# First batch's softmax sums moved from TensorE to GpSimd and VectorE, and the weight rounding spread over more slots, in a one-core attention and Fourier kernel

## The chip, the core and the metric

The kernel runs on one core of one Trainium2 chip. The core has five engines that work side by side, each through its own list of instructions in order: TensorE (PE: matrix products, results in PSUM), VectorE (DVE), ScalarE (ACT), GpSimd (POOL) and SyncE (SP, which here only issues transfers). An instruction that must wait for another engine holds up all behind it on its own engine. The metric is device time in microseconds; the kernel before takes 1061.83 us, the median of three runs (1060.62 to 1062.22).

## The reference

Inputs are q, k and v of 4 batches, 8 heads, 768 positions and 64 features, a table of sampled blocks, and two weight matrices of 512 x 2048 and 2048 x 512. For each batch and head:

```python
scores = scale * q @ k.T                     # 768 x 768
scores = where(mask, scores, -1e9)           # window, first and last block, 3 sampled blocks
attn = exp(scores - max) ; attn = attn / sum(attn)
x = attn @ v                                 # heads side by side: 768 x 512
mixed = real(fft over positions and features of x)
u = x + mixed ; un = normalised rows of u
out = u + maximum(un @ w_ch1, 0) @ w_ch2
```

## The kernel before, in words

Two heads make a pair; there are 16 pairs, four a batch. A pair is worked on in 12 units: two halves of 384 query positions, each with six chunks `c` of 128 key positions. For a unit TensorE makes the scores of both heads (`scores`, L573, 128 keys x 384 queries each), ScalarE takes their exponentials into a tile `e` (`weigh`, L593; four such tiles, 128 x 768), and TensorE multiplies `e` with v (`values`, L647). Two units are a slot, three slots a half pair, six a pair, 24 a batch (`SB`). `slot(sl)` writes the instructions of one slot: scores of this slot, values of the slot before, and what else fits. In the early slots the mask is added by four small TensorE products (L583); later VectorE multiplies with a mask tile instead (L603). The switch comes when the first batch's mixing has been written out.

The softmax sums. For the second batch and later, `gather` adds up the `e` tiles of a half pair into a tile `acc`: five additions, either one VectorE instruction (L628) or two GpSimd instructions, one per head (L633), whichever a small clock in the planner says is ready sooner. Per pair, `total` (L720 to L731) then lets TensorE sum `acc` over its partitions into a PSUM tile `sp`, and VectorE adds that to `sums` (`into_sums`, L696 and L698). For the first batch, `add_up` (L700 to L718) lets TensorE sum the `e` tiles themselves, in every slot, with eight-record products of 32 rows (L714), kept in PSUM over a half pair. `norm_steps` turns the sums over and inverts them.

The weights arrive as 64-bit floats in 32 chunks of 512 KB (`w_load`, L451, on SyncE's queue) into raw tiles and are rounded to 32 bits by `w_round`: two ScalarE instructions (L460, L463) and five VectorE instructions (L464, L466, L469, L471, L472). Five raw tiles ("rooms" 0, 1, 3, 4, 5 of a shared buffer) go around. `w_steps` writes `W_PACE * sl` roundings by slot `sl`. The same rooms later hold what the mixing needs: rooms 0 and 1 the folded x, rooms 2 and 3 the hidden activations, rooms 4 and 5 differences for a product scheme with seven multiplications instead of eight. SyncE's queue also carries q, k, v and the tables of cosines and sines, whose landing tiles VectorE frees by copying them out (L389, L414).

When a batch's attention is done, its mixing is written into the next batch's slots by `begin`: VectorE scales x (L756) and folds it (L779 to L807), TensorE transforms it (`along`, L827 to L855, writes `zp`; `across` writes `pq`), VectorE and GpSimd normalise, TensorE transposes (L970) and VectorE makes differences (L1007). Then the channel products (`quad`, L1045, and `channels`, L1101) are placed between attention slots. The planner keeps estimates of each engine's time in `when` and writes a step when it expects its inputs; nothing is reordered on the chip. PSUM tiles have tags: `s` (2, scores), `o` (1, values), `m` (2) and `t` (1). `add_up` uses `m`, `total` and the transposes `xt` (L670) and `tp` (L506) use `t`.

Of the kernel before, what the change touches and what calls it, by code (L numbers as in the profile page):

```python
# [11 lines left out]
FP32 = mybir.dt.float32  # L12
# [3 lines left out]
U32 = mybir.dt.uint32  # L16
AX = mybir.AxisListType
ALU = mybir.AluOpType
# [84 lines left out]
def kernel(  # L103
# [14 lines left out]
    nc = tc.nc  # L118

    B, H, S, D = q.shape  # L120
    DM = H * D
    FF = w_ch1.shape[1]
    P = 128
    C = S // P
    BLK = 32
    NB = S // BLK
    NR = sampled_blocks.shape[1]
    HS = S // 2
# [9 lines left out]
    NP = H // 2  # L138
# [20 lines left out]
    pick = const.tile([P, 2 * BLK], FP32, name="pick")  # L159
# [16 lines left out]
    sum_p = ctx.enter_context(tc.tile_pool(name="sum_p", bufs=1))  # L176
# [3 lines left out]
    un_p = ctx.enter_context(tc.tile_pool(name="un_p", bufs=3))  # L180
# [4 lines left out]
    ps_m = ctx.enter_context(tc.tile_pool(name="ps_m", bufs=2, space=PSUM))  # L185
# [3 lines left out]
    when = {"PE": 0.0, "ACT": 0.0, "DVE": 0.0, "POOL": 0.0}  # L189
    free = {"m": [0.0, 0.0], "t": [0.0]}  # L190

    def busy(engine, us, after=0.0):
        when[engine] = max(when[engine], after) + us
        return when[engine]

    def bank(tag):

        at = free[tag].index(min(free[tag]))
        when["PE"] = max(when["PE"], free[tag][at])
        free[tag][at] = float("inf")  # L200
        return tag, at

    def give(which, at):
        free[which[0]][which[1]] = at + HOP

    HOP = 0.1

    def room(i, shape, name, dtype=FP32):
        return big.tile(shape, dtype, tag=f"big{i}", name=name)

    pairs = [(b, j) for b in range(B) for j in range(NP)]
# [84 lines left out]
    def bit(n):  # L296
# [5 lines left out]
                      in_=bass.AP(tensor=_words(sampled_blocks, NB * NR), offset=0,  # L302
                                  ap=[[0, NB], [1, 2 * NB * NR]]))
# [132 lines left out]
    WN = 512  # L436
    wchunks = []
# [6 lines left out]
                              ap=[[2 * cols, P], [1, 2 * WN]])  # L444
                wchunks.append((src, w_sb[:, row, col:col + WN]))
    wraw = {}
    W_ROOMS = (0, 1, 3, 4, 5)

    def w_load(i):
        t = room(W_ROOMS[i % len(W_ROOMS)], [P, 3 * WN], "wraw", U32)  # L450
        nc.sync.dma_start(out=t[:, 0:2 * WN].bitcast(I32), in_=wchunks[i][0])  # L451
        wraw[i] = t

# [28 lines left out]
    by_pe, to_gather = set(), deque()  # L482
    masks = {"by_pe": True}

    turned, e_of, acc_of, o_of, sums_of, x_of, sp_of = {}, {}, {}, {}, {}, {}, {}
    s_at, e_at, e_free, oT_at, acc_at = {}, {}, {}, {}, {}

    def turn_on(n, a, half):
# [63 lines left out]
    UP = 2 * C  # L552
    UNITS = len(pairs) * UP
    SLOT = 2
# [32 lines left out]
    def weigh(u, s):  # L587
        n, w = divmod(u, UP)
        half, c = divmod(w, C)
        e = ep.tile([P, 2, HS], FP32, tag="e", name="e")  # L590
        e_of[u] = e
        if u in by_pe:
            nc.scalar.activation(out=e, in_=s[:, :, 0:HS], func=ACT.Exp, scale=scale)  # L593
            e_at[u] = busy("ACT", 0.8, max(s_at[u], e_free.pop(u - 2 * SLOT, 0.0))) + HOP
            if n >= NP:
                to_gather.append(u)

            if w >= UP - SLOT:
                gather_to(u)
        else:  # L600
            nc.scalar.activation(out=s[:, :, 0:HS], in_=s[:, :, 0:HS], func=ACT.Exp, scale=scale)  # L601
            m = mask[:, c, half * HS:(half + 1) * HS].rearrange("p (o s) -> p o s", o=1)
            nc.vector.tensor_tensor(out=e, in0=s[:, :, 0:HS], in1=m.broadcast_to([P, 2, HS]),  # L603
                                    op=ALU.mult)
            e_at[u] = busy("DVE", 0.97, busy("ACT", 0.8, s_at[u]) + HOP) + HOP
            gather_to(u)
            if n >= NP:
                gather(u)
# [5 lines left out]
    def gather(u):  # L614


        n, w = divmod(u, UP)
        half, c = divmod(w, C)
        if c == 0:
            return  # L620
        if c == 1:
            acc_of[n, half] = acc_p.tile([P, 2, HS], FP32, tag="acc", name="acc")
        acc, e = acc_of[n, half], e_of[u]
        start = e_of[u - 1] if c == 1 else acc
        at = max(e_at[u], acc_at.get((n, half), 0.0))
        sooner = max(when["DVE"], at) + 1.0 < max(when["POOL"], at) + 2.9
        if u in by_pe and masks["by_pe"] and w < UP - SLOT and sooner:
            nc.vector.tensor_tensor(out=acc, in0=start, in1=e, op=ALU.add)  # L628
            acc_at[n, half] = busy("DVE", 1.0, at) + HOP
        else:  # L630

            for i in range(2):
                nc.gpsimd.tensor_add(out=acc[:, i, :], in0=start[:, i, :], in1=e[:, i, :])  # L633
            acc_at[n, half] = busy("POOL", 2.9, at) + HOP
        e_free[u] = acc_at[n, half]

    def values(u):
# [51 lines left out]

    def into_sums(key, j, sp):  # L690
        if j == 0:
            if key == (0, 1):
                sums_of[key] = un_p.tile([P, DM], FP32, tag="un", name="sums")[:, 0:HS]
            else:
                sums_of[key] = sum_p.tile([P, HS], FP32, tag="sums", name="sums")
            nc.vector.tensor_copy(out=sums_of[key], in_=sp)  # L696
        else:
            nc.vector.tensor_tensor(out=sums_of[key], in0=sp, in1=sums_of[key], op=ALU.add)  # L698

    def add_up(us):  # L700


        n, w = divmod(us[0], UP)
        half, c = divmod(w, C)
        j = pairs[n][1]
        if c == 0:
            sp_of[n, half] = ps_m.tile([P, 512], FP32, tag="m", name="sp"), bank("m")
        sp, at = sp_of[n, half]
        sp = sp[:, 0:HS]
        busy("PE", 0.85)  # L710
        for r, u in enumerate(us):
            for i in range(2):
                g = BLK * (2 * i + r)
                nc.tensor.matmul(sp[g:g + BLK, :], pick[:, BLK - j:2 * BLK - j], e_of[u][:, i, :],  # L714
                                 start=(c == 0), stop=(c == C - SLOT), tile_position=(0, g))
        if c == C - SLOT:
            into_sums((0, half), j, sp)
            give(at, busy("DVE", 0.6, when["PE"] + HOP))  # L718

    def total(n):  # L720

# [11 lines left out]
    def norm_steps(b):  # L733

        r = sm.tile([P, T, 4, NP], FP32, tag="r", name="r", bufs=2)

        def invert(half):
            sums = sums_of.pop((0, half) if b == 0 else b)
            st = ps_t.tile([P, T, 4, BLK], FP32, tag="t", name="st")
            for c in range(T):  # L740
                nc.tensor.transpose(st[:, c, :, :].rearrange("p g r -> p (g r)"),
                                    sums[:, c * P:(c + 1) * P], ident)
            if b > 0:
                nc.vector.reciprocal(out=r, in_=st[:, :, :, 0:NP])
                return
            for i in range(2):
                to = r[:, :, 2 * half + i, :]
                nc.vector.tensor_copy(out=to, in_=st[:, :, 2 * i, 0:NP])
                nc.vector.tensor_tensor(out=to, in0=st[:, :, 2 * i + 1, 0:NP], in1=to, op=ALU.add)
            if half == 1:  # L750
                nc.vector.reciprocal(out=r, in_=r)

        def scale_x(half, c):
            xc = x_of[b, half][:, c, :].rearrange("p (j i d) -> p j i d", i=2, d=D)
            rc = r[:, c, 2 * half:2 * half + 2, :].rearrange("p i (j o) -> p j i o", o=1)
            nc.vector.tensor_tensor(out=xc, in0=xc, in1=rc.broadcast_to([P, NP, 2, D]),  # L756
                                    op=ALU.mult)

        return ([("t", lambda h=h: invert(h), 0.45, 0.0, 0.9) for h in range(2 if b == 0 else 1)] +
                [("d", lambda h=h, c=c: scale_x(h, c), 0.0, 0.0, 0.9)  # L760
                 for h in range(2) for c in range(T)])

# [484 lines left out]
    LEAVES = 9.0  # L1247
    SP = UP // SLOT
    SB = SP * NP
    W_PACE = 1.42  # L1250
    short, apart, late, due = deque(), deque(), deque(), deque()
    asked = set()
    needed = set()
    state = {"paired": False, "total": None, "w": 0, "got": 0, "owed": 0.0, "ready": 0.0}
# [89 lines left out]
        return True  # L1344

    def w_loads():
        while state["got"] < min(len(wchunks), state["w"] + len(W_ROOMS)):
            w_load(state["got"])
            state["got"] += 1

# [5 lines left out]
    def slot(sl):  # L1356
        phase, r = divmod(sl, SB)
# [6 lines left out]
        def sum_up():  # L1364

            at = due.popleft()
            done = range(SLOT * at, SLOT * at + SLOT)
            for u in done:
                values(u)
            if at < SB:  # L1370
                add_up(done)
            for u in done:
                e_of.pop(u)

# [47 lines left out]
        if sl < B * SB and n % NP == 1 and s == 1:  # L1422
# [3 lines left out]
                until(lambda: (b - 2, 1) in finished)  # L1426
                at = when["PE"] + LEAVES
            short.append(("t", at, lambda: place(n - 1, 1)))
        if sl > SB and s == 0 and sl <= B * SB:
            short.append(("t", acc_at[n - 1, 1], lambda: total(n - 1)))  # L1430
            state["total"] = short[-1]
        if r == 0:
# [186 lines left out]
```

## Time and profile before

| what | value |
|---|---|
| median of three runs | 1061.83 us (1060.62 to 1062.22) |
| profiled execution: span, first to last instruction | 1059.7 us |
| profiled execution: its own device time | not given beside the span |
| TensorE busy | 1036.7 us, mean granted clock 0.995 |
| VectorE, ScalarE, GpSimd busy | 654.7, 374.3, 235.6 us |
| slots 3 to 24 (20.63 to 123.33 us) | 102.70 us: TensorE busy 99.25, VectorE 92.87, ScalarE 88.36, GpSimd 0.00 |
| slots 24 to 33 (123.33 to 158.00 us) | 34.67 us: TensorE 34.18, VectorE 31.81, ScalarE 20.79, GpSimd 24.18 |

A line of the timeline gives the start in us from the span's start, the duration, the engine, the line of the kernel, the operation, the tiles (written, then read), the shape, how many instructions were merged, and in brackets the idle time before it with what ended it. TensorE's float products are recorded twice each, so eight records stand for four products. A line of a table by stretches gives the stretch, its length, busy time and instructions of TensorE, TensorE's weight loads, VectorE, ScalarE and GpSimd, then the granted TensorE clock, the transfers' share and GB/s.

### The profile page before, as it was taken

The page shows a single profiled execution, that of the slowest core. Times are in us where ns is not written, and L with a number is a line of the kernel's source. Part 1 is how long each engine was busy: PE and PEld are TensorE (multiplying, and loading weights), DVE is VectorE, ACT ScalarE, POOL GpSimd, SP SyncE. Part 2 cuts the span into 40 slices and gives each one's busy share as a digit, 9 for nine tenths or more (in the row PEclk, how much of TensorE's full clock was granted, in tenths as well). Part 3 has the DMA queues.
Part 4 walks back from the last instruction along what each step waited for, and adds up shares of the span by engine and source line. Part 5 has one row for each costly group of instructions (what it writes and reads, how often), then busy time and mean ns, then how long its engine had stood idle before and what let it go on. Part 6 is the DMA issues. An engine that isn't in the chain of part 4 may idle for free.

```text
span 1059.7 us, 12422 instructions
## 1 busy us (share of the span) xinstructions
PE 1036.7 (98%) x4390; PEld 535.8 (51%) x4390; DVE 654.7 (62%) x1218; ACT 374.3 (35%) x742; POOL 235.6 (22%) x262
## 2 busy tenths in 40 slices
PE   8999999999999999999999999999999999999996
PEld 4333345444455554444444555444445554578575
DVE  6898894667645445664668364765457455575663
ACT  6978855664030112342441302253220211210210
POOL 1000183537000002454553001256520001000000
PEclk9999999999999999999999999999999999999998
DMA  7757422220000002212220001221000001000001
GB/s 214 231 168 232 117 46 45 45 47 15 1 0 1 1 0 48 59 29 54 42 54 2 1 0 30 60 38 28 11 11 6 1 0 32 29 0 1 1 20 43
DMA packets 120803, 46.65 MB, mean 44 GB/s; under 512 B 108176, under 2 KB 113822, under 8 KB 120734
## 3 DMA queue, kind: packets, MB, share of 16 engines
q1 hardware_dynamic: 119484, 45.06, 17.3%
q10 hardware_dynamic: 1218, 0.72, 0.3%
q8 instruction: 36, 0.59, 0.2%
q14 instruction: 33, 0.27, 0.1%
q0 software_dynamic: 32, 0.01, 0.0%
HBM read 37.11 MB, written 6.29 MB: 41 GB/s over the span
## 4 chain that ended last, share of the span: by engine, by line
PE 89%; DVE 4%; DMA 3%; ACT 2%; issue 1%; SPq 0%; POOL 0%; ACTq 0%; DVEq 0%
PE y L1101 23%; PE z L1045 15%; PE s L573 12%; PE o L647 10%; PE yp L1045 7%; PE yy L1164 7%; PE xp L1045 4%; PE zp L855 2%; DMA out_dram<-x 1%; PE s L583 1%; PE zp L827 1%; PE sp L714 1%; PE sp L728 1%; PE utp L970 1%; PE xt L670 1%
## 5 line engine op out<-in xcount | busy, mean ns | idle before, releaser
L633 POOL TENSOR_TENSOR acc<-acc,e 128x384 f32<-128x384 f32 x158 | 159.3, 1042 | 94.1 <-DVE e L603 75.1
L573 PE MATMUL s<-qT,kT 64*128 64x384 f32 x768 | 154.0, 516 | 7.7 <-ACT e L593 4.3
L647 PE MATMUL o<-e,vr 128*64 128x384 f32 x768 | 141.8, 497 | 0.0
L1101 PE MATMUL y<-w_sb,hB 128*128 128x512 f32 x288 | 128.2, 596 | 1.0 <-DVE x L1104 1.0
L1101 PE MATMUL y<-w_sb,hA 128*128 128x512 f32 x288 | 128.4, 595 | 0.0
L603 DVE TENSOR_TENSOR e<-s,mask 128x768 f32<-128x768 f32 x92 | 83.8, 951 | 57.6 <-ACT s L601 47.8
L1104 DVE TENSOR_TENSOR x<-y,x 128x512 f32<-128x512 f32 x72 | 49.7, 690 | 110.9 <-PE y L1101 110.8
L573 PEld LDWEIGHTS s<-qT,kT 64*128 64x128 f32 x768 | 64.2, 186 | 85.8 <-issue 22.1
L601 ACT ACTIVATE s<-s 128x768 f32<-128x768 f32 x92 | 69.9, 792 | 87.5 <-PE s L573 87.0
L1045 PE MATMUL z<-unT,t 128*128 128x384 f32 x256 | 93.1, 486 | 1.2 <-DVE hA L1050 1.2
L633 POOL TENSOR_TENSOR acc<-e 128x384 f32<-128x384 f32 x42 | 47.1, 1142 | 211.6 <-ACT e L593 126.7
L1050 DVE TENSOR_TENSOR hA<-z,hA 128x384 f32<-128x384 f32 x64 | 35.7, 557 | 87.5 <-PE z L1045 87.5
L593 ACT ACTIVATE e<-s 128x768 f32<-128x768 f32 x100 | 76.1, 815 | 36.2 <-PE s L583 31.2
L1101 PEld LDWEIGHTS y<-w_sb,hB 128*128 128x128 f32 x288 | 53.4, 190 | 67.7 <-issue 65.0
L918 POOL TENSOR_SCALAR st<-st 128x1 f32<-128x1 f32 x24 | 8.6, 358 | 346.9 <-DVE st L917 346.8
L1101 PEld LDWEIGHTS y<-w_sb,hA 128*128 128x128 f32 x288 | 53.3, 190 | 62.8 <-issue 59.7
L647 PEld LDWEIGHTS o<-e,vr 128*64 128x64 f32 x768 | 47.9, 136 | 70.3 <-issue 67.9
L1054 ACT ACTIVATE hA<-hA 128x384 f32<-128x384 f32 x64 | 33.5, 523 | 120.3 <-DVE hA L1050 119.9
L1045 PEld LDWEIGHTS z<-unT,t 128*128 128x128 f32 x256 | 48.5, 190 | 35.5 <-DVE hA L1050 2.1
L1054 ACT ACTIVATE hB<-hB 128x384 f32<-128x384 f32 x64 | 33.5, 523 | 86.5 <-DVE hB L1050 84.2
L1065 ACT COPY hA<-xp 128x384 f32<-128x384 f32 x32 | 15.3, 478 | 97.9 <-PE xp L1045 97.9
L1045 PE MATMUL xp<-unT,w_sb 128*128 128x384 f32 x128 | 47.2, 492 | 0.0
(202 smaller groups left out, 1428.7 us busy)
## 6 DMA issues: line engine op xcount, KB each, us to landing
wraw<-in_moe_w_ch_dram SPq DMA_DIRECT2D x32, 512.0 KB
vr<-in_v_dram SPq DMA_DIRECT2D x30, 192.0 KB
qb<-in_q_dram SPq DMA_DIRECT2D x44, 96.0 KB
kb<-in_k_dram SPq DMA_DIRECT2D x44, 96.0 KB
x<-oT SPq DMA_DIRECT2D x192, 12.0 KB
out_dram<-x SPq DMA_DIRECT2D x15, 128.0 KB
out_dram<-x SPq DMA_DIRECT2D x7, 256.0 KB
qr<-in_q_dram SPq DMA_DIRECT2D x24, 64.0 KB
```

The lines of the kernel that those rows point to most:

```text
L573: nc.tensor.matmul(s[:, i, 0:HS], kT[rows, c * P:(c + 1) * P], qT[rows, queries], start=True, stop=u not in by_pe)
L593: nc.scalar.activation(out=e, in_=s[:, :, 0:HS], func=ACT.Exp, scale=scale)
L601: nc.scalar.activation(out=s[:, :, 0:HS], in_=s[:, :, 0:HS], func=ACT.Exp, scale=scale)
L603: nc.vector.tensor_tensor(out=e, in0=s[:, :, 0:HS], in1=m.broadcast_to([P, 2, HS]), op=ALU.mult)
L633: nc.gpsimd.tensor_add(out=acc[:, i, :], in0=start[:, i, :], in1=e[:, i, :])
L647: nc.tensor.matmul(o[D * i:D * i + D, :], vt[:, i, c, :], e[:, i, :], start=(c == 0), stop=(c == C - 1))
L1045: nc.tensor.matmul(to, a[:, k, :], c[:, k, :], start=(k == 0), stop=(k == ND // 2 - 1))
L1050: tt(out=to, in0=ps, in1=a, op=ALU.add)
L1054: nc.scalar.activation(out=h, in_=h, func=ACT.Relu)
L1101: nc.tensor.matmul(y, hs[0, half][:, l, m * P:(m + 1) * P], w2_sb[:, 4 * r + l, :], start=(l == 0), stop=(l == 3))
L1104: nc.vector.tensor_tensor(out=x[:, m, :], in0=y, in1=x[:, m, :], op=ALU.add)
L1164: nc.tensor.matmul(ps, a[:, k, :], c[k // 2][:, k % 2, :] if isinstance(c, list) else c[:, k, :], start=(k == 0), stop=(k == 3))
```

## The change

The first batch's sums are made like the others': `add_up` and its special cases go, every unit's `e` goes through `gather`, and `total` runs for every pair. The planner's price for a GpSimd addition goes from 2.9 to 2.2. The weight rounding goes from 1.42 chunks a slot to one, so it ends some eight slots into the second batch, and chunks from the twentieth on use only rooms 3, 4 and 5, since the mixing wants rooms 0 and 1 then.

```diff
     wraw = {}
-    W_ROOMS = (0, 1, 3, 4, 5)
+    W_FREE = 20
+    W_ROOMS = [(0, 1, 3, 4, 5)[i % 5] if i < W_FREE else (3, 4, 5)[(i - W_FREE) % 3]
+               for i in range(len(wchunks))]
...
             e_at[u] = busy("ACT", 0.8, max(s_at[u], e_free.pop(u - 2 * SLOT, 0.0))) + HOP
-            if n >= NP:
-                to_gather.append(u)
+            to_gather.append(u)
...
-        sooner = max(when["DVE"], at) + 1.0 < max(when["POOL"], at) + 2.9
+        sooner = max(when["DVE"], at) + 1.0 < max(when["POOL"], at) + 2.2
...
-            acc_at[n, half] = busy("POOL", 2.9, at) + HOP
+            acc_at[n, half] = busy("POOL", 2.2, at) + HOP
...
-    def add_up(us):
-        n, w = divmod(us[0], UP)
-        half, c = divmod(w, C)
-        j = pairs[n][1]
-        if c == 0:
-            sp_of[n, half] = ps_m.tile([P, 512], FP32, tag="m", name="sp"), bank("m")
-        sp, at = sp_of[n, half]
-        sp = sp[:, 0:HS]
-        busy("PE", 0.85)
-        for r, u in enumerate(us):
-            for i in range(2):
-                g = BLK * (2 * i + r)
-                nc.tensor.matmul(sp[g:g + BLK, :], pick[:, BLK - j:2 * BLK - j], e_of[u][:, i, :],
-                                 start=(c == 0), stop=(c == C - SLOT), tile_position=(0, g))
-        if c == C - SLOT:
-            into_sums((0, half), j, sp)
-            give(at, busy("DVE", 0.6, when["PE"] + HOP))
...
-            sums = sums_of.pop((0, half) if b == 0 else b)
+            sums = sums_of.pop(b)
...
-    W_PACE = 1.42
+    W_PACE = 1.0
...
     def w_loads():
-        while state["got"] < min(len(wchunks), state["w"] + len(W_ROOMS)):
+        while (state["got"] < len(wchunks) and
+               W_ROOMS[state["got"]] not in W_ROOMS[state["w"]:state["got"]]):
             w_load(state["got"])
...
-            if at < SB:
-                add_up(done)
...
-        if sl > SB and s == 0 and sl <= B * SB:
+        if 0 < sl <= B * SB and s == 0:
             short.append(("t", acc_at[n - 1, 1], lambda: total(n - 1)))
```

More of the change, by code (lines that the diff above doesn't have):

```diff
@@ L446 @@
     wraw = {}
-    W_ROOMS = (0, 1, 3, 4, 5)
+    W_FREE = 20
+    W_ROOMS = [(0, 1, 3, 4, 5)[i % 5] if i < W_FREE else (3, 4, 5)[(i - W_FREE) % 3]
+               for i in range(len(wchunks))]
     def w_load(i):
-        t = room(W_ROOMS[i % len(W_ROOMS)], [P, 3 * WN], "wraw", U32)
+        t = room(W_ROOMS[i], [P, 3 * WN], "wraw", U32)
         nc.sync.dma_start(out=t[:, 0:2 * WN].bitcast(I32), in_=wchunks[i][0])
@@ L483 @@
     masks = {"by_pe": True}
-    turned, e_of, acc_of, o_of, sums_of, x_of, sp_of = {}, {}, {}, {}, {}, {}, {}
+    turned, e_of, acc_of, o_of, sums_of, x_of = {}, {}, {}, {}, {}, {}
     s_at, e_at, e_free, oT_at, acc_at = {}, {}, {}, {}, {}
@@ L691, in into_sums @@
         if j == 0:
[L692 to L695, printed above, removed]
+            sums_of[key] = sum_p.tile([P, HS], FP32, tag="sums", name="sums")
             nc.vector.tensor_copy(out=sums_of[key], in_=sp)
@@ L735, in norm_steps, with invert @@
         r = sm.tile([P, T, 4, NP], FP32, tag="r", name="r", bufs=2)
-        def invert(half):
-            sums = sums_of.pop((0, half) if b == 0 else b)
+        def invert():
+            sums = sums_of.pop(b)
             st = ps_t.tile([P, T, 4, BLK], FP32, tag="t", name="st")
@@ L742, in invert @@
                                     sums[:, c * P:(c + 1) * P], ident)
[L743 to L751, printed above, removed]
+            nc.vector.reciprocal(out=r, in_=st[:, :, :, 0:NP])
         def scale_x(half, c):
@@ L757, in scale_x @@
                                     op=ALU.mult)
-        return ([("t", lambda h=h: invert(h), 0.45, 0.0, 0.9) for h in range(2 if b == 0 else 1)] +
+        return ([("t", invert, 0.45, 0.0, 0.9)] +
                 [("d", lambda h=h, c=c: scale_x(h, c), 0.0, 0.0, 0.9)
```

## The prediction

> **What bounds the kernel now.** I read the page's busy shares, then the timelines of TensorE, VectorE and GpSimd in the first batch, then the longest stall there.
>
> ```profile
> PE 1036.7 (98%) x4390; PEld 535.8 (51%) x4390; DVE 654.7 (62%) x1218; ACT 374.3 (35%) x742; POOL 235.6 (22%) x262
> 85.46 1.56 PE L573 MATMUL s<-qT,kT 64*128 64x384 f32 x8
> ...
> 87.75 1.51 PE L647 MATMUL o<-e,vr 128*64 128x384 f32 x8
> 89.19 0.85 PE L714 MATMUL sp<-e,pick 128*32 128x384 f32 x8
> 89.98 1.56 PE L573 MATMUL s<-qT,kT 64*128 64x384 f32 x8
> ...
> 99.59 0.59 PE L573 MATMUL s<-qT,kT 64*128 64x384 f32 x2 [0.20 <-ACT e L593]
> ```
>
> TensorE is busy 98%, so on paper every removed matmul counts. One slot's sums (L714) cost 0.785 us, from 89.19 to the next start at 89.98. Three slots take 14.1 us (85.46 to 99.59), 4.7 a slot.
>
> ```profile
> 18.75 0.43 DVE L464 TENSOR_SCALAR wraw<-wraw 128x512 uint32<-128x512 uint32 x1 [2.25 <-ACT wraw L463]
> 19.21 0.69 DVE L466 SCALAR_TENSOR_TENSOR w_sb<-wraw 128x512 uint32<-128x512 uint32 x1
> 19.93 0.43 DVE L469 TENSOR_SCALAR wraw<-w_sb 128x512 uint32<-128x512 uint32 x1
> 20.39 0.69 DVE L471 TENSOR_TENSOR wraw<-wraw 128x512 f32<-128x512 f32 x1
> 21.12 0.69 DVE L472 TENSOR_TENSOR w_sb<-w_sb,wraw 128x512 f32<-128x512 f32 x1
> 21.73 0.42 DVE L464 TENSOR_SCALAR wraw<-wraw 128x512 uint32<-128x512 uint32 x1
> ```
>
> This is one weight chunk: five instructions, 2.98 us (18.75 to 21.73), three of them with two tensors as input. GpSimd is idle until 126.75. There its first adds meet the last chunk:
>
> ```profile
> 126.75 1.10 POOL L633 TENSOR_TENSOR acc<-e 128x384 f32<-128x384 f32 x1 [121.65 <-ACT e L593]
> 127.81 1.44 POOL L633 TENSOR_TENSOR acc<-e 128x384 f32<-128x384 f32 x1
> 127.03 1.37 DVE L471 TENSOR_TENSOR wraw<-wraw 128x512 f32<-128x512 f32 x1
> 128.43 1.37 DVE L472 TENSOR_TENSOR w_sb<-w_sb,wraw 128x512 f32<-128x512 f32 x1
> 131.17 1.00 POOL L633 TENSOR_TENSOR acc<-acc,e 128x384 f32<-128x384 f32 x1 [1.92 <-ACT e L593]
> 132.12 0.99 POOL L633 TENSOR_TENSOR acc<-acc,e 128x384 f32<-128x384 f32 x1
> ```
>
> The reader is to see L471 and L472 at 1.37 instead of 0.69 us, and an add at 1.44 instead of 1.00: the two engines take turns, one pair per 1.40 us (127.03 to 128.43). Alone an add half repeats every 0.955 us (131.17 to 132.12; the next two starts are 133.08 and 134.03) and L471 every 0.73, 1.685 together, so a turn saves 0.285.
>
> ```profile
> 70.01 2.46 PE L573 MATMUL s<-qT,kT 64*128 64x384 f32 x8 [2.40 <-ACT e L593]
> 68.06 0.66 ACT L460 ACTIVATE wraw<-wraw 128x512 f32<-128x512 uint32 x1 [3.29 <-DMA wraw<-in_moe_w_ch_dram]
> 58.49 1.15 SPq L384 DMA_DIRECT2D tab<-in_cos_s_dram  x2
> 67.60:76.11 8.51, 6.11 (x34) 2.39 (x31) 7.45 (x20) 8.05 (x15) 0.00 (x0) 0.80 0.94 310
> ```
>
> This is how a late VectorE reaches TensorE: SyncE's queue stood until 58.49 for a table buffer that VectorE frees, weight loads queued behind it, ScalarE waited 3.29 us for one of them, its exponentials behind that, and TensorE 2.40; the granted clock then fell (0.80 in this stretch, eight score matmuls in 2.46 us).
>
> **The change, part by part.** TensorE loses 24 sums x 0.785 = 18.8 us and one set of three transposes, 0.5. It gains four per-pair sums (L728: 182.00 to 182.79, 0.79), 3.1. In the changed order the first mixing is late, so four more slots (100 units before, 108 after) get their mask by TensorE: 4 slots x 0.42 (L583, 184.18 to 184.60) = 1.7. Net 14.5 less. VectorE loses eight mask products (0.95 each) and some 3 us of sums and ratios, hidden under TensorE's products.
>
> Five of six units per half pair need an add. In the changed order 39 of the first batch's 40 adds stand on GpSimd, one on VectorE: 78 halves where GpSimd was idle, ten per three slots. The rounding goes from 1.42 chunks a slot to one, so it lasts to slot 32 instead of 23.
>
> Per three slots, slots 3 to 24, after the change:
> - TensorE: 14.1 - 3 x 0.785 + half of 0.785 = 12.2 us, 4.05 a slot.
> - VectorE alone: 3 x 2.98 + 1.1 (tables, 0.74 per two slots) + 0.3 = 10.3, 3.4 a slot.
> - GpSimd alone: 10 x 0.955 = 9.6, 3.2 a slot.
> - GpSimd and VectorE taking turns: 9.55 + 8.94 - 10 x 0.285 = 15.6, 5.2 a slot.
>
> The last is the largest. It holds if all five rounding instructions exclude an add; if only the three with two inputs do (0.72 + 0.73 + 0.61 = 2.06), it is 9.55 + 6.18 - 9 x 0.285 = 13.2, 4.4 a slot. No row shows L464 or L469 waiting, but the add beside L469 took 1.10 instead of 1.00. I take 5.2; the ends are 4.05 (no conflict) and 5.6 (table copies also exclude, 0.3 to 0.4 a slot).
>
> The Trainium skill, "SBUF — State Buffer", section "Who interferes with whom", says that VectorE and GpSimd share one pair of ports: an instruction with two SBUF inputs, or a copy or tensor_scalar in a two-port mode, and a GpSimd read exclude each other for the whole instruction. The 1.37 us rows agree for two inputs. Strictly, without the 0.285, it would give 18.5 / 3 = 6.2 a slot, and as an estimate a time of 1108; the trace's turns are shorter, and I go by them.
>
> A late VectorE has no slack to hide in. The new per-pair sum takes the one-buffer PSUM tile that the next slot's transposes (L670) need, and VectorE frees it (L698) only after the chunks queued ahead. The weight loads wait for VectorE too, with tables, q, k and v behind them on SyncE's queue. On GpSimd a late add holds one of four weight tiles `e`, for which ScalarE's next exponential waits. So VectorE can trail by about one slot.
>
> The sum, in the profiled execution's time (span 1059.7; its time outside the span isn't given; the median of the runs is 1061.83, 2.1 more, and I add the difference to that):
> - Slots 1 and 2: two sums gone, -1.6 (0 if conflict starts at once).
> - Slots 3 to 24 took 102.7 (20.63 to 123.33). After: 21 x 5.2 - 5.2 (the slot that VectorE may trail) = 104.0, +1.3. Ends: TensorE alone, 99.25 busy - 16.5 + 2.4 - 1.7 for the clock = 83.5, -19; at 5.6 a slot, +15.
> - Slots 24 to 33 took 34.7 (123.33 to 158.00). After: eight chunks 23.8, 30 halves 28.7, one scaling 0.7, less 30 x 0.285 = 44.6, +9.9. Ends: 0, and 53.2 without the saving, +18.5.
> - First mixing: from the last chunk to the last fold VectorE took 129.8 to 160.6, 30.8 us; less 2.2 idle and less 4.4 of work now done earlier or dropped (four ratio pairs and a reciprocal 1.8, a scaling 0.7, a transpose 0.95, an add 0.94), 24.2. TensorE's cover, five slots to its new place at slot 39, is 5 x 3.6 = 18. +6, ends 0 and 10.
> - In slot 53 the first product follows the last transposes with no attention between; it waits for VectorE's differences (L1007, 0.68 each; two, less products that need none): +1.5, ends 0 and 5.
> - Masks: +1.7. Extra weight loads beside q, k, v in slots 24 to 33: 0, the queue moves 49 GB/s at 128 to 161 us against 227 earlier; if that cover went, one 2.4 us stall. The eight chunks' 11.2 us on ScalarE (0.70 twice each) there: 0, it is busy 20.8 of 34.7; without that room they would add to each slot's exponentials, 1.25 a slot.
>
> From slot 55 the order is as before. Sum +18.8: 1080.6, say 1081. Low ends together give -18.9, high ends +50.
>
> **The rivals.**
> - No conflict worth the name: TensorE stays the bound, 1061.8 - 14.5 = 1047. For it: 98% busy, GpSimd idle. Against: the four conflict rows. It decides if turns cost under 4.05 a slot. Faster.
> - Only two-input instructions exclude: 21 x 4.4 - 4.4 = 88.0 (-14.7); then 8 x 2.06 + 28.7 + 0.7 - 25 x 0.285 = 38.8 (+4.1); with -1.6, +3, +1.5, +1.7 it is -6, 1056. For it: L469 never over 428 ns. Against: the 1.10 add. Faster.
> - Conflict and stalls add up: ScalarE waits on weights as at 68.06 and TensorE falls to half clock again; +15, +14, +8, +3, +1.7, -1.6 = +40, 1102. For it: the chain at 58 to 70 us. Against: one chunk a slot asks less of the loads.
>
> **How the numbers follow.** Chances: forecast 0.58 (alone 1062 to 1092), no conflict 0.14, two-input only 0.11, added stalls 0.17. The range 1053 to 1103 leaves out the no-conflict case (0.14) and some 0.06 above. Faster by over 0.2% (about what this measurement can tell): 0.14 + 0.10 + 0.01 = 0.25; within it 0.02; slower 0.73.
>
> **What would show it.** Right: L466, L471 and L472 well over 0.69 us in the first batch, adds near 1.4, slots of about 5.2 us to slot 32, TensorE idle some 20% there, waiting for exponentials or for the tile of L670. For the case that all five exclude: L464 and L469 above 0.43. Wrong: slots of 4.1 us and a busy TensorE; or a long wait at the first zp, which would put the loss in the mixing.

## The result and the profile after

The changed kernel takes 1104.4 us (median of 4 runs, 1102.1 to 1105.21) against 1061.53 us: a ratio of 1.040 (95% interval 1.0386 to 1.0415), 42.9 us slower. The forecast was 1081, with a range of 1053 to 1103. The sign was right and the size was not. One of the four executions of the kernel called "sums alone" below took 2129.88 us, against 1121.48 to 1122.79 of the other three, and is left out of its median.

First the busy line of the page and two stretches of the changed kernel, slots 3 to 24 and 24 to 33 (columns: TensorE, its weight loads, VectorE, ScalarE, GpSimd, then clock, transfer share, GB/s):

```profile
PE 1036.8 (94%) x4243; PEld 540.2 (49%) x4243; DVE 707.1 (64%) x1196; ACT 374.2 (34%) x742; POOL 340.7 (31%) x346
20.11:138.98 118.87, 93.80 (x521) 40.36 (x521) 106.92 (x144) 78.45 (x162) 84.46 (x71) 0.89 0.44 127
138.98:196.85 57.87, 37.44 (x209) 15.78 (x208) 56.25 (x63) 32.30 (x60) 41.47 (x34) 0.85 0.45 116
```

TensorE's matmul time is the same 1037 us although it has fewer products: some ran at half clock (0.89 and 0.85 of full speed granted as the mean of these two stretches). VectorE is busy 52 us more with fewer instructions. Slots 3 to 24 went from 102.7 to 118.9 us, slots 24 to 33 from 34.7 to 57.9.

Next one pair's end in the changed kernel, from the timelines of VectorE, GpSimd and TensorE:

```profile
72.97 1.23 DVE L466 TENSOR_SCALAR wraw<-wraw 128x512 uint32<-128x512 uint32 x1
74.23 1.37 DVE L468 SCALAR_TENSOR_TENSOR w_sb<-wraw 128x512 uint32<-128x512 uint32 x1
...
78.11 3.08 DVE L389 COPY cs_sb<-tab 128x128 f32<-128x128 f32 x7
81.11 0.41 DVE L466 TENSOR_SCALAR wraw<-wraw 128x512 uint32<-128x512 uint32 x1
...
84.08 0.55 DVE L696 TENSOR_TENSOR sums<-sp,sums 128x384 f32<-128x384 f32 x1
76.11 4.82 POOL L634 TENSOR_TENSOR acc<-acc,e 128x384 f32<-128x384 f32 x4 [1.06 <-ACT e L595]
75.13 1.51 PE L648 MATMUL o<-e,vr 128*64 128x384 f32 x8
84.68 0.90 PE L671 MATMUL xt<-ident,oT 128*128 128x128 f32 x3 [8.04 <-DVE sums L696]
85.51 2.93 PE L575 MATMUL s<-qT,kT 64*128 64x384 f32 x8
```

While GpSimd adds (to 80.93), VectorE's rounding instructions, such as L466 and L468, last 1.2 to 1.4 us instead of 0.43 and 0.69, and the seven table copies 3.08 instead of 0.74. Once GpSimd stops, L466 is back at 0.41. VectorE works through a whole chunk more before it reaches the pair's sums (L696) at 84.08; until then they hold the one PSUM tile of tag `t`, and TensorE, due there at about 76.6, stands 8.04 us. The next score products take 2.93 us instead of 1.56. This happens five times, once a pair (total us, times, longest):

```profile
PE xt L671 <- DVE sums L696: 22.2, 3, 8.0
PE xt L671 <- DVE sums L694: 14.3, 2, 7.8
```

That is 36.5 us in five waits, most of the 42.8 by which TensorE's idle time in the span has grown (23.0 to 65.8). In slots 24 to 33 VectorE is busy 97%, and the rounding's five instructions now cost this much each (busy and mean ns, then idle time):

```profile
L474 DVE TENSOR_TENSOR w_sb<-w_sb,wraw 128x512 f32<-128x512 f32 x10 | 11.2, 1116 | 0.3
L468 DVE SCALAR_TENSOR_TENSOR w_sb<-wraw 128x512 uint32<-128x512 uint32 x11 | 11.1, 1007 | 0.4
L473 DVE TENSOR_TENSOR wraw<-wraw 128x512 f32<-128x512 f32 x10 | 11.0, 1097 | 0.3
L471 DVE TENSOR_SCALAR wraw<-w_sb 128x512 uint32<-128x512 uint32 x10 | 9.2, 916 | 0.3
L466 DVE TENSOR_SCALAR wraw<-wraw 128x512 uint32<-128x512 uint32 x11 | 8.4, 766 | 0.2
```

The means add up to 4.9 us a chunk instead of 2.98, and ten or eleven chunks fall into these nine slots, not eight: VectorE had finished only 20 of the 32 when slot 24 began.

### The profile page after: what moved, and what is told of

It reads as the page before. It is cut to its first block, busy times and chain, and to the rows that moved or that the text cites. A ratio compares the mean times of both kernels' runs of the same rounds, so it can differ in the third digit from the quotient of the medians.

```text
span 1102.6 us, 12245 instructions
## 1 busy us (share of the span) xinstructions
PE 1036.8 (94%) x4243; PEld 540.2 (49%) x4243; DVE 707.1 (64%) x1196; ACT 374.2 (34%) x742; POOL 340.7 (31%) x346
## 4 chain that ended last, share of the span: by engine, by line
PE 81%; DVE 9%; issue 3%; ACT 3%; POOL 2%; DMA 1%; SPq 1%; DVEq 0%; ACTq 0%; POOLq 0%
PE y L1071 22%; PE z L1015 15%; PE s L575 10%; PE o L648 8%; PE yp L1015 7%; PE yy L1134 6%; PE xp L1015 4%; POOL acc L634 2%; PE zp L825 1%; DVE wraw L473 1%; DVE w_sb L468 1%; DVE t L977 1%; DVE wraw L471 1%; PE zp L797 1%; DVE wraw L466 1%
## 5 line engine op out<-in xcount | busy, mean ns | idle before, releaser
L634 POOL TENSOR_TENSOR acc<-acc,e 128x384 f32<-128x384 f32 x228 | 248.6, 1124 | 124.1 <-DVE e L604 64.7
L575 PE MATMUL s<-qT,kT 64*128 64x384 f32 x768 | 160.0, 535 | 8.0 <-ACT e L595 4.5
L1071 PE MATMUL y<-w_sb,hB 128*128 128x512 f32 x288 | 128.5, 597 | 1.4 <-DVE x L1074 1.4
L1071 PE MATMUL y<-w_sb,hA 128*128 128x512 f32 x288 | 128.4, 595 | 0.0
L575 PEld LDWEIGHTS s<-qT,kT 64*128 64x128 f32 x768 | 67.4, 194 | 87.8 <-issue 25.7
L604 DVE TENSOR_TENSOR e<-s,mask 128x768 f32<-128x768 f32 x84 | 76.4, 950 | 48.9 <-ACT s L602 39.1
L595 ACT ACTIVATE e<-s 128x768 f32<-128x768 f32 x108 | 81.9, 812 | 45.0 <-PE s L585 33.1
L634 POOL TENSOR_TENSOR acc<-e 128x384 f32<-128x384 f32 x56 | 62.9, 1144 | 108.4 <-PE sp L706 86.5
L602 ACT ACTIVATE s<-s 128x768 f32<-128x768 f32 x84 | 63.7, 792 | 84.7 <-PE s L575 84.6
L1020 DVE TENSOR_TENSOR hA<-z,hA 128x384 f32<-128x384 f32 x64 | 35.7, 557 | 87.6 <-PE z L1015 87.6
L1071 PEld LDWEIGHTS y<-w_sb,hB 128*128 128x128 f32 x288 | 53.3, 190 | 67.8 <-issue 65.4
L1071 PEld LDWEIGHTS y<-w_sb,hA 128*128 128x128 f32 x288 | 53.3, 190 | 62.8 <-issue 59.5
L1015 PE MATMUL z<-t,w_sb 128*128 128x384 f32 x128 | 46.8, 488 | 3.0 <-DVE t L977 3.0
```

The source lines that it names most:

```text
L575: nc.tensor.matmul(s[:, i, 0:HS], kT[rows, c * P:(c + 1) * P], qT[rows, queries], start=True, stop=u not in by_pe)
L1015: nc.tensor.matmul(to, a[:, k, :], c[:, k, :], start=(k == 0), stop=(k == ND // 2 - 1))
L1020: tt(out=to, in0=ps, in1=a, op=ALU.add)
L1071: nc.tensor.matmul(y, hs[0, half][:, l, m * P:(m + 1) * P], w2_sb[:, 4 * r + l, :], start=(l == 0), stop=(l == 3))
```

## The experiments

The theory: GpSimd's adds and VectorE's instructions exclude each other, so VectorE falls behind, and TensorE waits for what VectorE frees. The rivals: the slower rounding is the loss; the order of VectorE's list is, whatever GpSimd does; GpSimd's own speed is; TensorE's clock is. All times are medians; "first y" is the start of the first channel product (L1101, or L1071 after), a milestone behind which little changes (790 to 793 us are left in every kernel of the table).

| kernel | us | ratio to before (95%) | slots 3-24 | slots 24-33 | first y |
|---|---|---|---|---|---|
| before | 1061.5 to 1062.3 | | 102.7 | 34.7 | 267.5 |
| changed | 1104.4 | 1.0386 to 1.0415 | 118.9 | 57.9 | 312.4 |
| pace alone | 1083.3 | 1.0175 to 1.0209 | 97.0 | 46.1 | 290.5 |
| sums alone | 1121.8 | 1.055 to 1.0592 | 144.5 | 52.7 | 326.7 |
| one add of five | 1065.3 | 1.0025 to 1.0048 | 86.2 | 47.7 | 272.9 |
| sums in `m` | 1099.4 | 1.0324 to 1.036 | 117.0 | 45.3 | 307.5 |
| filled waits | 1101.3 | 1.0355 to 1.039 | 115.9 | 57.1 | 309.4 |
| adds on VectorE | 1090.7 | 1.0248 to 1.0283 | 107.3 | 50.0 | 298.7 |
| short rounding | 1050.0 | 0.9873 to 0.9906 | 86.4 | 35.7 | 257.8 |
| before, pace 1.3 | 1074.6 | 1.010 to 1.0134 | 102.9 | 41.4 | 280.8 |
| before, short rounding | 1056.3 | 0.9927 to 0.996 | 97.0 | 34.6 | 261.0 |
| pace alone, free tail | 1067.4 | 1.0033 to 1.0067 | 97.0 | 36.7 | 274.9 |
| tables on ScalarE | 1098.1 | 1.032 to 1.0354 | 114.3 | 57.7 | 306.4 |
| before, tables on ScalarE | 1060.2 | 0.9972 to 0.9992 | 100.6 | 34.7 | 265.6 |

**Each part alone.** First the pace on the kernel before:

```diff
-    W_ROOMS = (0, 1, 3, 4, 5)
+    W_FREE = 20
+    W_ROOMS = [(0, 1, 3, 4, 5)[i % 5] if i < W_FREE else (3, 4, 5)[(i - W_FREE) % 3]
+               for i in range(len(wchunks))]
...
-    W_PACE = 1.42
+    W_PACE = 1.0
...
```

> The kernel before with only the slower weight rounding (one chunk a slot, to slot 32, three rooms from chunk 20 on); the first batch's sums stay on TensorE. Conflict theory (GpSimd's adds and VectorE's rounding take turns at something shared): no conflict in slots 0 to 24, eight chunks meet the second batch's adds in slots 24 to 33, so +5 to +20, 1067 to 1082. Rival, the pace itself is the loss (rounding and mixing come too late): most of the +43 is here, 1090 or more. Third possibility, pace is free: 1058 to 1064.

Measured +21. Two stretches of this kernel, slots 3 to 24 and 24 to 33:

```profile
20.96:117.92 96.96, 96.96 (x670) 40.04 (x666) 70.35 (x158) 78.46 (x162) 0.00 (x0) 1.00 0.56 160
117.92:164.06 46.14, 36.71 (x212) 15.63 (x211) 43.05 (x61) 31.51 (x58) 26.03 (x22) 0.93 0.53 135
```

In the first batch the slower pace is better by 5.7 us: TensorE never waits. Beside the second batch's adds, slots 24 to 33 take 11.5 us more than in the kernel before, and from slot 33 to the first y another 16.9 are lost. Then the sums alone, at the old pace and with the old rooms:

```diff
...
-    W_PACE = 1.0
+    W_PACE = 1.42
...
```

> The changed kernel with the rounding's old pace (1.42 chunks a slot, five rooms): only the sums are moved. Conflict theory: VectorE needs 1.42 x 2.98 + 0.45 = 4.7 us a slot alone and ten waits of up to 0.67 per three slots besides, so it is later in the first batch than in the changed kernel and done earlier; total much the same, 1090 to 1115. Rival, the slower pace is the loss: 1070 or less.

Measured +60.1, above the expected span: the moved sums are the larger loss, and the slower pace, a loss by itself, takes 17 us off it. With 1.42 chunks a slot VectorE is later still: slots 3 to 24 hold 135.5 us of its work, against 106.9 in the changed kernel. The two parts don't add up (21 + 60 against 43).

**Is it GpSimd beside VectorE?** Three kernels change one side of the meeting, and a fourth is the control for one of them. Four of five adds left out:

```diff
+        if n < NP and c > 1:
+            e_free[u] = at
+            return
```

> The changed kernel, but in the first batch only the first of the five adds of a half pair is made; the other four are left out, so the first batch's sums are of two units of six. Conflict theory: with 16 add halves instead of 78 beside the rounding, VectorE keeps up (3.4 us a slot against TensorE's 4.05), the five waits of 6 to 8 us for the sums' PSUM tile shrink to one or two, 1055 to 1075. Rival, the order of VectorE's queue alone makes the sums late whatever GpSimd does: five waits stay, 1090 or more.

This kernel's first stretch (slots 3 to 24):

```profile
18.94:105.11 86.17, 83.62 (x521) 36.96 (x521) 74.63 (x150) 78.51 (x162) 17.82 (x14) 1.00 0.64 180
```

1065.3: 39 us back with 62 add halves gone. VectorE's list keeps its order through slot 24, so the order alone is not the cause; without the conflict the first batch runs at TensorE's speed (86.2 us for 21 slots, 4.1 a slot). Slots 24 to 33, where the second batch's adds meet the rounding's end, still cost 13 us more than in the kernel before (47.7). Next the rounding shortened instead:

```diff
-        nc.scalar.mul(out=lo.bitcast(FP32), in_=lo, mul=2.0 ** -52)
...
-        nc.vector.tensor_scalar(out=a, in0=dst.bitcast(U32), scalar1=0xFF800000, scalar2=None, ...)
-        nc.vector.tensor_mul(out=a.bitcast(FP32), in0=lo.bitcast(FP32), in1=a.bitcast(FP32))
-        nc.vector.tensor_add(out=dst, in0=dst, in1=a.bitcast(FP32))
```

> The changed kernel with the low words' part of the rounding left out (ScalarE's L462 and VectorE's L471, L473, L474): weights are cut to 20 fraction bits instead of rounded; two VectorE instructions a chunk are left of five, 1.15 us of 2.98. Conflict theory: the turns cost 9.55 + 3.45 - 1.7 = 11.3 us per three slots, under TensorE's 12.2, so TensorE is the bound again, the waits for the sums go, 1045 to 1060. Rival, GpSimd's own speed and its hold on the weight tiles is the loss: adds as before, 1085 or more.

1050.0, 54 us back, with all adds in place. GpSimd's speed and its hold on the weight tiles `e` are therefore not the bound. This kernel's first stretch (slots 3 to 24):

```profile
19.44:105.80 86.36, 83.48 (x523) 37.18 (x522) 64.79 (x90) 66.82 (x141) 74.85 (x71) 1.00 0.64 187
```

TensorE is busy 97% at full clock with GpSimd busy 87%. It is faster than the kernel before, but with weights cut to 20 fraction bits, so it is no fair rival. The same cut in the kernel before (L460, L469, L471 and L472) tells what the whole change is worth when VectorE has room:

```diff
-        nc.scalar.mul(out=lo.bitcast(FP32), in_=lo, mul=2.0 ** -52)
...
-        nc.vector.tensor_add(out=dst, in0=dst, in1=a.bitcast(FP32))
```

> The kernel before with the low words' part of the rounding left out as in the run of the changed kernel with short rounding (weights cut to 20 fraction bits; two VectorE instructions a chunk instead of five), sums on TensorE. If the moved sums are worth TensorE's 14.5 us once VectorE has room, this is 10 to 15 us above that run's 1050: 1058 to 1063. Rival, the short rounding itself made that run fast: 1045 to 1052.

1056.3, a little under the expected 1058 to 1063: with short rounding the whole change gains 6.3 us, against 14.5 us of products taken off TensorE. With the full rounding it loses 42.9. Last, the adds on VectorE:

```diff
-        if u in by_pe and masks["by_pe"] and w < UP - SLOT and sooner:
+        if n < NP or (u in by_pe and masks["by_pe"] and w < UP - SLOT and sooner):
```

> The changed kernel with the first batch's 40 adds all on VectorE (one instruction of 0.95 us instead of two GpSimd halves). Conflict theory: VectorE's need is 3.4 + 5 x 0.95 / 3 = 5.0 us a slot without any turn-taking, a little under the 5.8 measured with it, so 1085 to 1100. Rival, GpSimd's own speed and its hold on the four weight tiles is the loss: with VectorE's quicker adds 1060 to 1075.

1090.7, 13.7 less than with GpSimd. Two groups of VectorE's instructions between 20 and 130 us:

```profile
L629 DVE TENSOR_TENSOR acc<-acc,e 128x768 f32<-128x768 f32 x30 | 28.6, 955 | 1.0
...
L474 DVE TENSOR_TENSOR w_sb<-w_sb,wraw 128x512 f32<-128x512 f32 x22 | 15.2, 692 | 0.7
```

The rounding is back at 692 ns. So an add that VectorE makes itself costs VectorE less than one that GpSimd makes beside it. Here 37 adds are 35.3 us, 0.95 each. In the changed kernel the 144 instructions of VectorE's first stretch take 106.9 us, with 71 add halves beside them; in the kernel with one add of five the same 144 take 71.1 (19.41 to 101.89 us there), with 14. That is 35.8 us for 28.5 adds, 1.26 each.

**Where the lateness lands.** The sums' tile from the other tag:

```diff
-        sp, at = ps_t.tile([P, HS], FP32, tag="t", name="sp"), bank("t")
+        pool, tag = (ps_m, "m") if n <= NP else (ps_t, "t")
+        sp, at = pool.tile([P, 512], FP32, tag=tag, name="sp")[:, 0:HS], bank(tag)
```

> The changed kernel with the per-pair sums of the first five pairs in a PSUM tile of tag m (two buffers) instead of t (one). Tile theory (VectorE's lateness costs so much because it is collected at one tile, in lumps that halve TensorE's clock): the five lumps go, the lateness shows in smaller waits, half clock falls from 48 us to under 20, 1080 to 1095. Rival, VectorE is simply the bound and any wait is as dear as another: 1100 to 1106, the lumps appear elsewhere.

1099.4, only 5 us back and not within either span, though 0.6 us from the rival's. The waits for the sums are gone; the wait of ScalarE for weight loads grows from 8.2 us in three times to this (again total us, times, longest):

```profile
ACT wraw L462 <- DMA wraw<-in_moe_w_ch_dram: 26.7, 6, 8.9
```

The lateness is collected elsewhere, as the rival had it. VectorE is busy 114.0 of the 117.0 us of slots 3 to 24: it is the bound, and the tile is only the place. Then TensorE kept busy through the five waits:

```diff
+        if half == 1 and n <= NP:
+            warm(26)
         xt, at = ps_t.tile([P, 512], FP32, tag="t", name="xt"), bank("t")
```

> The changed kernel with 26 dummy 128x128 products (some 6.5 us at full clock) on TensorE ahead of each of the five transposes that wait for VectorE's sums. Clock theory: TensorE keeps its clock through the waits, 48 us at half clock fall to under 15, and 10 to 20 us come back, 1085 to 1095. Rival, VectorE is the bound and TensorE's clock hides behind it: 1100 to 1108.

The mean granted clock rises from 0.976 to 0.993, and 3.1 us come back, as the rival had it (1101.3). The half clock hides behind VectorE. Behind the fifth wait the dummy products end 3.5 us after the sums, so the test may have cost a little itself.

**The tables.** Their copies (L389) given to ScalarE:

```diff
-        nc.vector.tensor_copy(
+        nc.scalar.copy(
```

> The changed kernel with the six sine and cosine tables copied out by ScalarE instead of VectorE (36 small instructions). In the changed kernel they took 13.4 us of VectorE instead of 4.1. If each small VectorE copy waits for a GpSimd add and that lateness adds up, up to 13 us come back: 1090 to 1098. Rival, VectorE's lateness is made up elsewhere, or ScalarE's in-order list holds the exponentials up instead: 1102 to 1108.

1098.1, 6.3 back, at the near end of what was expected; of VectorE's first 130 us the copies vanish, and the rounding meets more of the adds instead (L471's mean rises from 678 to 874 ns). The same edit in the kernel before, whose copies stand at the same line:

```diff
-                nc.vector.tensor_copy(
+                nc.scalar.copy(
```

> The kernel before with the six tables copied out by ScalarE instead of VectorE and nothing else: a try at a version that beats both kernels. VectorE has 4.1 us less to do in the first batch, where a late VectorE held up the weight loads at 58 to 70 us. If that lateness is what TensorE waits for there, the 2.40 us wait and the half clock after it shrink: 1056 to 1060. Rival, ScalarE's in-order list makes the exponentials late instead, or the wait is the transfers' own: 1061 to 1066.

1060.2, a ratio of 0.9982 (0.9972 to 0.9992): just past the near end of what was expected, and the fastest of the kernels that round the weights in full. Its line for 60 to 80 us, and that of the kernel before:

```profile
60.00:80.00 20.00, 19.52 (x134) 8.06 (x132) 18.87 (x33) 18.80 (x52) 0.00 (x0) 1.00 0.89 262
```

```profile
60.00:80.00 20.00, 17.60 (x110) 7.17 (x107) 18.41 (x45) 14.26 (x28) 0.00 (x0) 0.91 0.69 216
```

The half clock (a mean of 0.91 in the second line) and the 2.40 us wait are gone.

**What of the pace costs.** The rounding's last eight chunks copied by ScalarE alone, in the kernel with the pace alone:

```diff
+        if i >= 24:
+            nc.scalar.copy(out=dst, in_=hi.bitcast(FP32))
+            return
```

> The pace-alone kernel (slower rounding, sums on TensorE) with the last eight chunks, those of slots 25 to 32, merely copied by ScalarE in one instruction, so these weights are not rounded; the order of all else is the same. If the +21 of the pace alone is the eight chunks' work on VectorE beside the second batch's adds, 1056 to 1064. Rival, the mixing being written six slots later is the loss by itself: 1075 to 1083.

1067.4, between the two spans: of the +21 of the pace, 16 go with the eight chunks' work on VectorE beside the second batch's adds, and 5 are left. These 5 are roughly a balance: slots 3 to 24 gain 5.7, slots 24 to 33 lose 2.1, and from slot 33 to the first y 10.8 are lost, which may be the later mixing (TensorE's four extra masked slots are 1.7 of it). That was argued and not tested.

And a pace between, in the kernel before:

```diff
-    W_PACE = 1.42
+    W_PACE = 1.3
```

> The kernel before with a rounding pace of 1.3 chunks a slot instead of 1.42 and nothing else: VectorE needs 3.9 + 0.45 us a slot instead of 4.7 against slots of 4.7, and is done about two slots later (slot 25). If the wait of 2.40 us at 70 us and the half clock after it come from VectorE's lateness, they go and the late end costs little: 1055 to 1060. Rival, any rounding past slot 23 costs as in the pace-alone run (+21 for eight chunks, 2.6 a chunk): 1063 to 1068.

1074.6, dearer than expected: slots 3 to 24 don't gain (102.9), and a rounding that ends two slots later already costs 12 us. The trace shows where: four chunks are left at slot 24 instead of two, VectorE is busy 38.4 of the 41.4 us of slots 24 to 33, and between slot 24 and the first y TensorE stands 5.9 us until VectorE has read the turned sums (L749) and 3.3 for a masked tile (L603), waits that are 0 and 0.4 us in the kernel before. Why two chunks make that much was not settled.

## Why the prediction was right in kind and wrong in size

Right: the direction; the mechanism (the turns, with the signs named for the case that all five instructions exclude: L466 and L471, the former L464 and L469, reach 1.24 us); that TensorE's 14.5 us are buried under VectorE (with the short rounding 6.3 of them come out); and the waits for the tile of L670, now L671. The adds fell short of the sign named for them: their median up to the end of the rounding is 1.19 us, not near 1.4. The Trainium skill's rule in "SBUF — State Buffer", section "Who interferes with whom", that a copy or tensor_scalar in a two-port mode excludes GpSimd too, agrees with the 1.23 and 3.08 us rows, though no run here shows the mode; that the other blocks for the whole instruction agrees less well, since a rounding instruction beside an add takes 1.37 and not the 0.69 + 0.955 = 1.65 of both.

Wrong, by the terms of the sum (medians and spans both differ by 42.9):

| term | predicted | measured |
|---|---|---|
| slots 1 and 2 (start of slot 3: 20.63 to 20.11) | -1.6 | -0.5 |
| slots 3 to 24 | +1.3 | +16.2 |
| slots 24 to 33 | +9.9 | +23.2 |
| first mixing, first product, masks (all behind slot 33) | +9.2 | +4.0 |

The step that failed is "VectorE can trail by about one slot". It took 5.2 us off the first stretch and charged them nowhere. VectorE finished 20 chunks there, two fewer than in the kernel with the pace alone, and ten or eleven fell into slots 24 to 33, which were reckoned with eight: at 4.9 us each, two to three chunks more are 10 to 15 us, about the 13.3 by which that term is off.

The first stretch is off by 14.9, and there the overlap failed: the sum let VectorE work without a break, but the stretch is 118.9 us with VectorE busy 106.9. While TensorE stood, ScalarE stood behind it in the copy of `xt` (25.1 us in three waits), so the next chunk's scaling came late (VectorE waited 9.2 us for ScalarE's L465), and GpSimd had no new tiles to add (35.0 us of waits for `e`). Three groups of VectorE's instructions in that stretch:

```profile
L466 DVE TENSOR_SCALAR wraw<-wraw 128x512 uint32<-128x512 uint32 x19 | 14.4, 756 | 9.2 <-ACT wraw L465 9.2
...
L389 DVE COPY cs_sb<-tab 128x1 f32<-128x1 f32 (+2 forms) x21 | 7.0, 400 | 0.0
L389 DVE COPY sn_sb<-tab 128x128 f32<-128x128 f32 (+2 forms) x15 | 6.5, 494 | 0.0
```

That VectorE's 106.9 us lie near the sum's 21 x 5.2 = 109 is partly luck. The rounding alone took 89.8 us for 20 chunks, 4.5 each, less than 5.2; the table copies, which the sum put at 0.3 to 0.4 us a slot and only into the upper end, went from 4.1 to 13.4. The profile of the kernel before had a row for this, a copy of 128x2 that takes 0.16 us and once, beside an add, 0.96 (minimum, median and maximum in ns):

```profile
L791 DVE COPY e<-x x4: 159/161/962, 152.5 to 809.9; 128x2 f32<-128x2 f32 x4
```

A term put at 0 came too, the extra weight loads in slots 24 to 33. ScalarE waited 8.2 us for them in three times; at the longest, TensorE stood as well:

```profile
148.46 0.67 ACT L462 ACTIVATE wraw<-wraw 128x512 f32<-128x512 uint32 x1 [4.32 <-DMA wraw<-in_moe_w_ch_dram]
150.43 2.93 PE L575 MATMUL s<-qT,kT 64*128 64x384 f32 x8 [3.97 <-ACT e L595]
```

A shared resource's sum of needs is a lower bound for a ring of engines that wait for each other, and I used it as the time. The rival "added stalls" (1102) came out nearest, but not by the half clock it leaned on: with the clock kept up, 1101.3.

## What to carry to other kernels

Before moving work from a full engine to an idle one, look for a row in which the idle engine's instruction meets those of the third engine that runs there, and add up what the two need in turns; here 78 add halves on an idle GpSimd cost more than the 18.8 us of products that they replaced. When an engine is reckoned to trail, charge the lag to the stretch where it is paid, and ask who stands while it is. Work that is put off into a stretch with the same conflict isn't hidden there: the pace that helped the first batch by 5.7 us cost 21 in all.

## What was not expected of the hardware

A short instruction can lose as much in a turn as a long one: table copies of 0.14 to 0.23 us alone reached 1.07 us beside GpSimd's adds, and rounding instructions of 0.69 us reached 1.38 to 1.55. A TensorE clock raised from 0.976 to 0.993 by dummy products was worth 3 us where VectorE set the pace.
